# Reordering the first pieces of work of an attention and mixture kernel, and dropping a pause of three steps later on

## The chip, the cores and the metric

The kernel runs on one core of one Trainium2 chip. The time is the device time of one execution in microseconds (us). Five engines matter: TensorE (PE in the rows) multiplies matrices, VectorE (DVE), ScalarE (ACT) and GpSimd (POOL) work element by element, and SyncE (SP, SPq for its queue) starts the transfers of the DMA engines. Each engine executes its own list of instructions in a fixed order and waits, at the head of that list, for what the next instruction needs.

## The reference, cut to what matters

Inputs: q, k, v of shape (8, 8, 576, 64), p of shape (8, 8, 32, 64); weights of two feed-forward stages. All float32.

```python
def sm_attn(qq, kk, vv):
    s = scale * np.matmul(qq, kk.transpose(0, 1, 3, 2))
    s = s - np.max(s, axis=-1, keepdims=True)
    a = np.exp(s)
    a = a / (np.sum(a, axis=-1, keepdims=True) + 1e-09)
    return np.matmul(a, vv)
p_packed = sm_attn(p, k, v)              # packing: 32 rows a head
out = sm_attn(q, p_packed, p_packed)     # spreading: 576 rows a head
x = out.transpose(0, 2, 1, 3).reshape(4608, 512)
h = x @ w_in                             # 512 -> 2048
x = (h * (1.0 / (1.0 + np.exp(-h)))) @ w_out
a = x @ w1                               # 512 -> 1024
b = x @ w2
h = a * b @ w3
return h @ w_out2                        # 1024 -> 512
```

## The kernel before, in words

Stage 1 does attention and the first feed-forward part, batch by batch; stage 2, from about 826 us on, does the second part with factors that were stored in DRAM. This text touches two places: the start, before TensorE has its steady flow of products, and the first 100 us of stage 2.

**The start.** The string `START` (L70 to L76) lists pieces of work in the order in which the program records them, up to each `|`. `P0` and `P1` are steps of the packing of batch 0 and batch 1 (`Pack.steps`): scores into `ps_s` (L318), maximum (L449, L450), exponential (L454), transposes into `ps_t` (L467), their copies `e`, the product `ps_o` (L318), its scaled copies `pk` on ACT (L491), the transpose `pkT` on DVE (L496) and the blocks `sbd` on POOL (L268). `S0` and `S1` are steps of `Spread` (from L600) for one half of batch 0's rows: transpose of the scores (L606), maximum (L610), subtraction (L611), exponential (L614), sums (L617 to L619), multiplication (L620), transpose back `sT` (L625), and the split of it into `a2`. The spread of `S0` is marked `early`.

`F` is one step of the weight decoder: the weights come in as 64-bit words, and class `Decode` turns one 128x512 piece into floats with two copies on ACT (`ps_dec`, `raw`, by way of L82), two instructions on DVE (L190, L192) and an addition on POOL (L196). `L` starts the load of a piece (L214). The buffers of the pieces go round, so a load waits until POOL's addition of an earlier piece has ended. The first eight pieces (`zi`) are of the first weight matrix, those behind them (`z`) of the second. `D` is `direct0`: two matrix products (L700) of `zi` with batch 0's packed rows `mbd` into one PSUM bank `ps_m0`, which is split into the slots `mq`: the high part is a copy on ACT (L82), the low part a subtraction on DVE (L91). Once `a2` and `mq` are there, a loop over items runs: `ps_h` (L98 to L100), then sg (L882), gg (L887), gh and gl, then `ps_x`.

Each number that is multiplied is carried as two parts, high and low: `split_hi` is a copy on ACT (L82), `split_lo` a subtraction on DVE or POOL (L91).

A scheduler then sets each engine's final order. `tc.issue_after(behind[x])` (in `hold`, L104) tells it that an instruction is not to stand ahead of the recorded instruction `behind[x]`. `act_on` (from L806) runs the tokens; it holds an `F` behind the latest `sg` and `gg`, once there are any.

**Stage 2.** `emit_ab` records, per step, products of left and right factors into `ps_a`, `ps_b` and `ps_e` (L1393), sums of them on DVE (`y`, L1424), and `o_steps` (L1554) multiplies the results by `w`, with sums on DVE (`o`, L1536). A generator of side work, `first_group`, is advanced between them: `second_right_factors` prepares the factors `w` from `zz` in four rounds (`mp` 0 to 3), then `right_sums(1)` forms the sums `xt`, `x2r`, `zz` on POOL (L1206) for the next group of rows, and these are split into `xct` and `xcb`. The last right factors are needed when the next group starts at about 920 us. Before round `mp` = 2 there are three bare `yield`s (L1305, L1306).

## Time and profile before

| | |
|---|---|
| device time, median of three runs | 1382.71 us (1380.78 to 1382.86) |
| the profiled execution: its own time | 1379.92 us |
| its span in the trace | 1378.1 us |
| PE busy | 1348.4 us, 98% of the span, 9161 instructions |
| DVE busy | 933.8 us, 68% |
| POOL busy | 902.3 us, 65% |
| ACT busy | 728.5 us, 53% |
| mean granted clock of TensorE | 0.998 of full |
| bytes moved | 272.94 MB, 198 GB/s in the mean |

The span runs from the first to the last instruction of the trace; the execution's own time is 1.82 us longer. A share of busy time is a mean over the whole span. The first slice of 40 has PE at 7 tenths, the others are at 8 or 9 and above; how much an engine waits in a stretch is read from the rows of that stretch.

### The profile page before, as it was taken

Reading aid. Unit: us, or ns where it says so; the run is one execution under the profiler, and the core shown is the slowest. Engines: PE = TensorE matmul, PEld = TensorE weight load, DVE = VectorE, ACT = ScalarE, POOL = GpSimd, SP = SyncE. Lnnn points to the kernel's source line nnn. Section 1 sums busy time; section 2 is a strip of 40 time slices with the busy share of each in tenths; the row PEclk is TensorE's granted clock in tenths of the full one; section 3 lists DMA queues with packets and bytes.
Section 4 is the critical chain, followed back from the end, with each engine's and each line's share of the span. In section 5 each row is a group of like instructions: output and inputs, shape, how many; then the busy total and the mean of one; then the engine's idle time right before and its main releaser. Section 6 shows DMA issues by size and latency. Waiting matters only on the chain.

```text
span 1378.1 us, 26479 instructions
## 1 busy us (share of the span) xinstructions
PE 1348.4 (98%) x9161; PEld 1306.8 (95%) x9161; DVE 933.8 (68%) x1622; ACT 728.5 (53%) x1633; POOL 902.3 (65%) x866
## 2 busy tenths in 40 slices
PE   7899999999999999999999999999999999999998
PEld 5688899999999999999999999999999999999998
DVE  5874747369665578767669748885775757757665
ACT  5855756465675566665556636443334433333432
POOL 2875967666889677888567544593755747646632
PEclk9999999999999999999999999999999999999999
DMA  9588757534676454865547648656667576576751
GB/s 322 187 297 263 242 165 224 166 120 150 224 235 192 144 157 126 268 206 152 197 137 246 194 159 304 214 169 199 220 185 237 169 213 218 169 218 203 214 161 54
DMA packets 191557, 272.94 MB, mean 198 GB/s; under 512 B 18752, under 2 KB 112320, under 8 KB 191424
## 3 DMA queue, kind: packets, MB, share of 16 engines
q1 hardware_dynamic: 173168, 251.20, 58.5%
q10 hardware_dynamic: 18256, 20.06, 4.2%
q8 instruction: 73, 1.20, 0.4%
q14 instruction: 60, 0.49, 0.1%
HBM read 209.06 MB, written 62.13 MB: 197 GB/s over the span
## 4 chain that ended last, share of the span: by engine, by line
PE 84%; DVE 6%; ACT 3%; POOL 2%; DMA 2%; issue 2%; SPq 1%; DVEq 0%; ACTq 0%; POOLq 0%
PE ps_a L1393 13%; PE ps_o L1554 12%; PE ps_x L100 8%; PE ps_x L98 8%; PE ps_x L99 8%; PE ps_e L1393 7%; PE ps_h L98 4%; PE ps_h L100 4%; PE ps_h L99 4%; PE ps_b L1393 3%; PE ps_w L99 1%; PE ps_w L98 1%; PE ps_w L100 1%; PE ps_m L99 1%; PE ps_m L98 1%
## 5 line engine op out<-in xcount | busy, mean ns | idle before, releaser
L98 PE MATMUL ps_x<-gh,wo 128*128 128x288 f32 x1024 | 301.8, 297 | 1.3 <-DVE xs L924 1.3
L99 PE MATMUL ps_x<-gh,wo 128*128 128x288 f32 x1024 | 300.4, 295 | 0.0
L100 PE MATMUL ps_x<-gl,wo 128*128 128x288 f32 x1024 | 293.7, 298 | 0.0
L91 POOL TENSOR_TENSOR gl<-gg,gh 128x288 fp32r<-128x288 f32 x256 | 232.4, 910 | 83.1 <-ACT gh L82 62.0
L887 DVE SCALAR_TENSOR_TENSOR gg<-sg,ps_h 128x288 f32<-128x288 f32 x256 | 114.8, 448 | 177.6 <-ACT sg L882 109.2
L1536 DVE TENSOR_TENSOR o<-o,ps_o 128x768 f32<-128x768 f32 x137 | 130.0, 950 | 97.2 <-PE ps_o L1554 94.6
L98 PEld LDWEIGHTS ps_x<-gh,wo 128*128 128x128 f32 x1024 | 192.1, 188 | 3.9 <-DVE xs L924 1.5
L99 PEld LDWEIGHTS ps_x<-gh,wo 128*128 128x128 f32 x1024 | 192.3, 188 | 1.9 <-issue 1.1
L91 POOL TENSOR_TENSOR mq<-mr,mq 128x256 fp32r<-128x256 f32 x168 | 140.4, 837 | 79.1 <-DVE mq L830 43.9
L100 PEld LDWEIGHTS ps_x<-gl,wo 128*128 128x128 f32 x1024 | 188.6, 188 | 3.0 <-issue 2.2
L82 ACT ACTIVATE gh<-gg 128x288 fp32r<-128x288 f32 x256 | 113.0, 442 | 92.1 <-DVE gg L887 86.7
L882 ACT ACTIVATE sg<-ps_h 128x288 f32<-128x288 f32 x256 | 103.6, 405 | 107.1 <-PE ps_h L100 82.7
L98 PE MATMUL ps_h<-a,mq 128*128 128x288 f32 x512 | 154.6, 302 | 1.6 <-DVE gg L887 1.6
L100 PE MATMUL ps_h<-a,mq 128*128 128x288 f32 x512 | 151.8, 297 | 0.0
L99 PE MATMUL ps_h<-a,mq 128*128 128x288 f32 x512 | 151.4, 296 | 0.0
L91 POOL TENSOR_TENSOR lfa<-y,lfa 128x384 fp32r<-128x384 f32 x69 | 78.7, 1140 | 83.2 <-ACT lfa L82 73.9
L1554 PE MATMUL ps_o<-w,lfs 128*128 128x256 f32 x828 | 118.5, 282 | 0.0
L1393 PE MATMUL ps_a<-xct,ws 128*128 128x384 f32 x576 | 116.0, 335 | 0.0
L1554 PEld LDWEIGHTS ps_o<-w,lfs 128*128 128x128 f32 x828 | 112.2, 190 | 0.0
L98 PEld LDWEIGHTS ps_h<-a,mq 128*128 128x128 f32 x512 | 96.1, 188 | 7.1 <-DVE gg L887 2.9
L1393 PEld LDWEIGHTS ps_a<-xct,ws 128*128 128x128 f32 x576 | 99.9, 188 | 0.0
L99 PEld LDWEIGHTS ps_h<-a,mq 128*128 128x128 f32 x512 | 96.1, 188 | 3.4 <-issue 1.4
(225 smaller groups left out, 3177.9 us busy)
## 6 DMA issues: line engine op xcount, KB each, us to landing
ws<-w_d SPq DMA_DIRECT2D x192, 256.0 KB, 3.1
wa<-w_d SPq DMA_DIRECT2D x144, 256.0 KB, 3.0
mr<-m_d SPq DMA_DIRECT2D x144, 128.0 KB, 2.7
raw<-in_moe_w_dram SPq DMA_DIRECT2D x32, 512.0 KB, 4.6
w_d<-w12s ACTq DMA_DIRECT2D x56, 256.0 KB, 2.8
wz<-wi_d SPq DMA_DIRECT2D x48, 256.0 KB, 4.3
m_d<-ms SPq DMA_DIRECT2D x96, 128.0 KB, 3.2
x_d<-xs SPq DMA_DIRECT2D x20, 576.0 KB, 3.6
```

The costliest lines, as they stand in the source:

```text
L82: return A.activation(out=dst, in_=src, func=ACTF.Copy, scale=mul)
L91: (eng or V).tensor_tensor(out=lo, in0=src, in1=hi.bitcast(F32), op=ALU.subtract)
L98: T.matmul(out=dst, lhsT=wh, rhs=xh, start=start, stop=False)
L99: T.matmul(out=dst, lhsT=wl, rhs=xh, start=False, stop=False)
L100: return T.matmul(out=dst, lhsT=wh, rhs=xl, start=False, stop=stop)
L882: ins = A.activation(out=sg, in_=ps, func=ACTF.Tanh, scale=0.5)
L887: ins = V.scalar_tensor_tensor(out=gg, in0=sg, scalar=1.0, in1=ps, op0=ALU.add, op1=ALU.mult)
L1393: ins = T.matmul(out=bank, lhsT=w[:, kt, wp], rhs=xt[:, kt, xp], start=first and (kt, n) == (0, 0), stop=last and (kt, n) == (1, 2), skip_ ...
L1536: V.tensor_tensor(out=oacc[k], in0=oacc[k], in1=ps, op=ALU.add)
L1554: T.matmul(out=ps[:, t], lhsT=l[:, lp], rhs=w[:, wp], start=fresh and t != 1 and n == 0, stop=done and t != 0 and n == 2, skip_group_check ...
```

## The change

The first line of `START` that has `P0 P0 P0 P0` is put in another order, with the same nine `F`, eight `L` and two `D`. Three decodes now stand directly behind batch 0's packing, the first step of batch 1's packing stands between the two spread steps, and `D D` follows the fourth decode. Until `sg` exists, every `F` and every `P1` is held behind the latest recorded instruction of batch 0 on ACT (`first_a`) and on DVE (`first_v`). These are set by the copies `e` of batch 0's packing, by four places of the early spread and by `direct0`. The tile `sT` of the early spread comes from the pool of the gate tiles `gg` in place of the pool `work`. In stage 2 the three `yield`s go.

```diff
-        "P0 P0 P0 P0 P0.tail S0 S0 P1 F L F L S1.load S0 P1 F L F L D D P1 F L F L P1 F L F L F "
+        "P0 P0 P0 P0 P0.tail F L F L F L S0 P1 S0 F L S1.load S0 P1 D D F L P1 F L F L P1 F L F "
...
             for et, (r, cs) in zip(pts, self.PARTS):
-                split_hi(ep[0][0:r, cs], et)
+                x = split_hi(ep[0][0:r, cs], et)
+                if self.b == 0:
+                    behind.update(first_a=x.ins)
...
-            V.tensor_tensor(
+            x = V.tensor_tensor(
                 out=s, in0=s, in1=mx.unsqueeze(2).to_broadcast([128, n, 32]), op=ALU.subtract
             )
-            A.activation(out=s, in_=s, func=ACTF.Exp, scale=scale)
+            y = A.activation(out=s, in_=s, func=ACTF.Exp, scale=scale)
+            if self.early:
+                behind.update(first_v=x.ins, first_a=y.ins)
...
-            sT = work([128, n * 32], "sT")
-            V.transpose(out=sT, in_=s.rearrange("p k i -> p (k i)"))
+            if self.early:
+                sT = g_p.tile([128, HS], F32, tag="gg", name="sT", bufs=4)
+            else:
+                sT = work([128, n * 32], "sT")
+            x = V.transpose(out=sT, in_=s.rearrange("p k i -> p (k i)"))
             cols = slice(hv[0] * HS, hv[-1] * HS + HS)
-            split(a2[b][:, hg, 0, cols], a2[b][:, hg, 1, cols], sT, eng=G if self.early else V)
+            y = split_hi(a2[b][:, hg, 0, cols], sT)
+            split_lo(a2[b][:, hg, 1, cols], sT, a2[b][:, hg, 0, cols], G if self.early else V)
+            if self.early:
+                behind.update(first_v=x.ins, first_a=y.ins)
...
-        split(dst[:, :, 0], dst[:, :, 1], ps.rearrange("p (j f) -> p j f", j=4))
+        src = ps.rearrange("p (j f) -> p j f", j=4)
+        behind["first_a"] = split_hi(dst[:, :, 0], src).ins
+        behind["first_v"] = split_lo(dst[:, :, 1], src, dst[:, :, 0]).ins
...
-            with hold("sg", "gg") if token == "F" and "sg" in behind else ExitStack():
+            last = ("sg", "gg") if "sg" in behind else ("first_v", "first_a")
+            held = token == "F" or (token == "P1" and "sg" not in behind)
+            with hold(*[x for x in last if held and x in behind]):
                 act(token)
...
-            for _ in range(3 if mp == 2 else 0):
-                yield
```

The final order differs only in the first 88 us or so and between 826 and 930 us; in between and behind, every engine's list is the same.

**DVE at the second direct product.** Before, this piece of VectorE's list reads as follows. `zi2` and `zi3` are decoded weights, `mq_176<-ps_m0_470` is the low part of the second direct product, `sT` the transposes back of batch 0's spread.

```order
L190 TENSOR_SCALAR zi2_186<-ps_dec_491 128x512
L192 SCALAR_TENSOR_TENSOR raws_180<-ps_dec_491,raws_180 128x512
L620 TENSOR_TENSOR s2_352<-s2_352,sm_363 128x288
L190 TENSOR_SCALAR zi3_187<-ps_dec_520 128x512
L192 SCALAR_TENSOR_TENSOR raws_180<-ps_dec_520,raws_180 128x512
L476 TENSOR_REDUCE rs_392<-psum0_131 128x1
L477 RECIPROCAL rs_392<-rs_392 128x1
L496 STREAM_TRANSPOSE pkT_505<-pk_500 128x64
L625 STREAM_TRANSPOSE sT_417<-s2_343 128x288
L91 TENSOR_TENSOR mq_176<-ps_m0_470,mq_176 128x4x128
L625 STREAM_TRANSPOSE sT_421<-s2_352 128x288
```

And in the changed kernel:

```order
L189 TENSOR_SCALAR zi1_185<-ps_dec_422 128x512
L191 SCALAR_TENSOR_TENSOR raw_241<-ps_dec_422,raw_241 128x512
L633 STREAM_TRANSPOSE sT_437<-s2_374 128x288
L477 TENSOR_REDUCE rs_388<-psum1_132 128x1
L477 TENSOR_REDUCE rs_404<-psum0_131 128x1
L478 RECIPROCAL rs_388<-rs_388 128x1
L478 RECIPROCAL rs_404<-rs_404 128x1
L90 TENSOR_TENSOR mq_176<-ps_m0_470,mq_176 128x4x128
L189 TENSOR_SCALAR zi2_186<-ps_dec_475 128x512
L191 SCALAR_TENSOR_TENSOR raw_243<-ps_dec_475,raw_243 128x512
L189 TENSOR_SCALAR zi2_186<-ps_dec_491 128x512
```

The subtraction `mq_176<-ps_m0_470` now stands ahead of the decodes of `zi2` and `zi3`, where these stood ahead of it; both `sT` stand ahead of it.

**PE at the same product.** The same product on TensorE, whose second half is the last matrix product that the subtraction needs; before:

```order
L318 MATMUL ps_s_384<-rows1_194,pb_225 128x288 x2
L700 MATMUL ps_m0_470<-zi1_185,mbd_157 128x512
L318 MATMUL ps_s_387<-rows1_194,pb_225 128x288 x2
L467 MATMUL ps_t_426<-ident_60,e1_381 128x128 x3
L467 MATMUL ps_t_430<-ident_60,e1_381 96x128 x2
L318 MATMUL ps_o_475<-vz_229,e_425 128x256 x2
```

And in the changed kernel, up to the second half:

```order
L317 MATMUL ps_s_399<-rows1_194,pb_225 128x288 x2
L466 MATMUL ps_t_442<-ident_60,e1_393 128x128 x3
L466 MATMUL ps_t_446<-ident_60,e1_393 96x128 x2
L466 MATMUL ps_t_454<-ident_60,e1_409 128x128 x3
L466 MATMUL ps_t_458<-ident_60,e1_409 96x128 x2
L317 MATMUL ps_o_483<-vz_229,e_441 128x256 x2
L317 MATMUL ps_o_483<-vz_231,e_441 128x256
L711 MATMUL ps_m0_470<-zi1_185,mbd_157 128x512
```

Both halves of batch 1's transposes (`ps_t_442` to `ps_t_458`) now stand ahead of the second half of `ps_m0_470`; before, only one half of them did.

**SP at the loads of the next queries.** `kq` and `rows2` are the query rows that the spread `S1` needs. Before:

```order
L214 DMA raw_243<-in_moe_w_in_dram 128x512
L214 DMA raws_180<-in_moe_w_in_dram 128x512 x2
L115 DMA kq_414<-in_q_dram 128x2x288
L115 DMA rows2_192<-in_q_dram 128x2x288
L214 DMA raw_455<-in_moe_w_in_dram 128x512
L214 DMA raw_463<-in_moe_w_out_dram 128x512
```

And in the changed kernel:

```order
L213 DMA raw_243<-in_moe_w_in_dram 128x512
L213 DMA raws_180<-in_moe_w_in_dram 128x512 x2
L213 DMA raw_359<-in_moe_w_in_dram 128x512
L213 DMA raw_428<-in_moe_w_out_dram 128x512
L114 DMA kq_430<-in_q_dram 128x2x288
L114 DMA rows2_192<-in_q_dram 128x2x288
```

The two loads of queries moved behind two more loads of weights, which need freed buffers.

**POOL in stage 2.** Here `xt`, `x2r` and `zz` are the sums for the next group of rows, `w34_3` the last of the factors `w`, `xct` and `xcb` low parts of the right factors. Before:

```order
L1206 TENSOR_TENSOR xt_12751<-x2r_12379 128x768
L91 TENSOR_TENSOR lfa22_12652<-y122_12518,lfa22_12652 128x384
L91 TENSOR_TENSOR lfs3_12646<-tmp_12612,lfs3_12646 128x384
L91 TENSOR_TENSOR lfs2_12618<-tmp_12611,lfs2_12618 128x384
L1424 TENSOR_TENSOR tmp_12612<-y021_12393,tmp_12611 128x384
L1206 TENSOR_TENSOR x2r_12379<-x2r_12379 128x2x384
L91 TENSOR_TENSOR w34_3_12530<-zz_12254,w34_3_12530 128x256
L91 TENSOR_TENSOR lfa12_12649<-y021_12393,lfa12_12649 128x384
L91 TENSOR_TENSOR xct1_12789<-xt_12751,xct1_12789 128x2x384
L1206 TENSOR_TENSOR zz_12752<-x2r_12379,xt_12751 128x768
```

And in the changed kernel:

```order
L1221 TENSOR_TENSOR xt_12692<-x2r_12384 128x768
L90 TENSOR_TENSOR lfa22_12657<-y122_12525,lfa22_12657 128x384
L90 TENSOR_TENSOR lfs3_12651<-tmp_12616,lfs3_12651 128x384
L90 TENSOR_TENSOR lfs2_12622<-tmp_12615,lfs2_12622 128x384
L1437 TENSOR_TENSOR tmp_12616<-y021_12398,tmp_12615 128x384
L1221 TENSOR_TENSOR x2r_12384<-x2r_12384 128x2x384
L1221 TENSOR_TENSOR zz_12693<-x2r_12384,xt_12692 128x768
L90 TENSOR_TENSOR lfa12_12654<-y021_12398,lfa12_12654 128x384
L90 TENSOR_TENSOR xcb11_12767<-x2r_12384,xcb11_12767 128x2x384
L90 TENSOR_TENSOR lfs4_12647<-tmp_12616,lfs4_12647 128x384
```

The first `zz` moved up by three instructions: a `w34_3`, an `lfa12` and an `xct1` that stood between it and `x2r` now stand elsewhere.

## Rows read from the trace of the kernel before

**Rows 1.** Windows: busy us (instructions) of PE, PEld, DVE, ACT, POOL; clock, DMA share, GB/s.

```profile
15.89:55.67 39.78, 31.02 (x124) 21.47 (x125) 34.55 (x78) 34.42 (x86) 24.37 (x23) 0.96 0.71 244
...
80.00:122.00 42.00, 42.00 (x281) 38.22 (x280) 25.51 (x50) 25.05 (x56) 28.79 (x29) 1.00 0.82 265
```

**Rows 2.** Chain of waits that ended at 68 us: start, length in us, what.

```profile
57.64 1.31 POOL z L196
...
58.97 0.33 SPq L214
...
60.29 6.15 DMA kq<-in_q_dram
...
66.57 1.21 PE ps_s L318 x4
```

**Rows 3.** Timeline of ACT: start, us, engine, line, operation, [idle before <- releaser].

```profile
15.23 0.62 ACT L82 ACTIVATE ps_dec<-raws 128x512 f32<-128x512 f32 x1 [1.45 <-DMA raws<-in_moe_w_in_dram]
...
16.33 1.46 ACT L491 ACTIVATE pk<-ps_o,rs 32x128 f32<-32x128 f32 x4
...
27.86 0.50 ACT L454 ACTIVATE e<-ps_s,nb 128x288 f32<-128x288 f32 x1
...
31.36 0.75 ACT L82 ACTIVATE e<-ps_t 128x384 f32<-128x384 f32 x2
```

**Rows 4.** Timeline of DVE in the start.

```profile
15.89 0.69 DVE L190 TENSOR_SCALAR zi<-ps_dec 128x512 int32<-128x512 int32 x1 [1.71 <-ACT ps_dec L82]
...
35.41 0.68 DVE L192 SCALAR_TENSOR_TENSOR raws<-ps_dec,raws 128x512 int32<-128x512 int32 x1
...
37.02 0.43 DVE L625 STREAM_TRANSPOSE sT<-s 128x288 f32<-128x288 f32 x1
37.40 0.69 DVE L91 TENSOR_TENSOR mq<-ps_m,mq 128x512 fp32r<-128x512 f32 x1
...
55.67 0.45 DVE L887 SCALAR_TENSOR_TENSOR gg<-sg,ps_h 128x288 f32<-128x288 f32 x1
```

**Rows 5.** Timeline of PE in the start.

```profile
12.38 2.43 PE L318 MATMUL ps_o<-vr,e 128*128 128x256 f32 x10 [0.36 <-ACT e L82]
...
31.89 2.43 PE L318 MATMUL ps_o<-vz,e 128*128 128x256 f32 x10 [2.05 <-ACT e L82]
34.15 1.02 PE L700 MATMUL ps_m<-zi,mbd 128*128 128x512 f32 x2
```

**Rows 6.** Timeline of SP's queue: start, us, the issue of transfers.

```profile
23.75 0.55 SPq L115 DMA_DIRECT2D kq<-in_q_dram  x1
```

**Rows 7.** DMA issues: count, KB each, us to landing; 22 to 30, then 31 to 36 us.

```profile
kq<-in_q_dram SPq DMA_DIRECT2D x1, 288.0 KB, 7.6
...
raw<-in_moe_w_out_dram SPq DMA_DIRECT2D x2, 512.0 KB, 4.0
```

**Rows 8.** Windows of stage 2, columns as in rows 1.

```profile
920.00:928.00 8.00, 6.17 (x38) 5.15 (x36) 8.00 (x9) 3.10 (x6) 8.00 (x6) 1.00 0.45 133
```

**Rows 9.** Waits of PE, 900 to 940 us: total us, times, longest.

```profile
PE ps_a L1393 <- DVE y L1424: 0.8, 1, 0.8
PE ps_o L1554 <- DVE o L1536: 0.8, 1, 0.8
PE ps_e L1393 <- DVE xcb L91: 0.3, 1, 0.3
```

**Rows 10.** Timeline of DVE in stage 2.

```profile
915.00 2.70 DVE L91 TENSOR_TENSOR xct<-zz,xct 128x768 fp32r<-128x768 f32 x1 [1.15 <-ACT xct L82]
...
918.91 0.54 DVE L1424 TENSOR_TENSOR y<-p,ps_a 128x384 f32<-128x384 f32 x1
919.49 1.62 DVE L1424 TENSOR_TENSOR y<-y,y 128x384 f32<-128x384 f32 x1
```

**Rows 11.** Timeline of POOL in stage 2.

```profile
899.49 2.16 POOL L1206 TENSOR_TENSOR xt<-x2r 128x768 f32<-128x768 f32 x1
...
912.24 1.85 POOL L1206 TENSOR_TENSOR zz<-x2r,xt 128x768 f32<-128x768 f32 x1
```

More of the change, by code (lines that the diff above doesn't have):

```diff
@@ L85, in split_hi @@
         if on_vector:
-            V.tensor_copy(out=hi, in_=src)
-        else:
-            act_copy(hi, src)
+            return V.tensor_copy(out=hi, in_=src)
+        return act_copy(hi, src)
     def split_lo(lo, src, hi, eng=None):
-        (eng or V).tensor_tensor(out=lo, in0=src, in1=hi.bitcast(F32), op=ALU.subtract)
+        return (eng or V).tensor_tensor(out=lo, in0=src, in1=hi.bitcast(F32), op=ALU.subtract)
     def split(hi, lo, src, on_vector=False, eng=None):
@@ L619, in steps @@
             V.reciprocal(out=sm, in_=sm)
-            V.tensor_tensor(
+            x = V.tensor_tensor(
                 out=s, in0=s, in1=sm.unsqueeze(2).to_broadcast([128, n, 32]), op=ALU.mult
             )
+            if self.early:
+                behind.update(first_v=x.ins)
             yield
-            sT = work([128, n * 32], "sT")
-            V.transpose(out=sT, in_=s.rearrange("p k i -> p (k i)"))
+            if self.early:
[3 more added lines that the diff above has]
+            x = V.transpose(out=sT, in_=s.rearrange("p k i -> p (k i)"))
             cols = slice(hv[0] * HS, hv[-1] * HS + HS)
-            split(a2[b][:, hg, 0, cols], a2[b][:, hg, 1, cols], sT, eng=G if self.early else V)
+            y = split_hi(a2[b][:, hg, 0, cols], sT)
+            split_lo(a2[b][:, hg, 1, cols], sT, a2[b][:, hg, 0, cols], G if self.early else V)
+            if self.early:
+                behind.update(first_v=x.ins, first_a=y.ins)
             yield
```

## The prediction

> **What bounds the kernel now.** I read the page's shares first (PE busy for 98% of the span), then windows, to find where PE is not full. There are two places in reach of the change. In the first, the start, the reader is to see that from 15.89 to 55.67 us PE is busy 31.02 of 39.78 us and loses 8.76, while DVE is busy 34.55 and ACT 34.42 [rows 1]. Both are nearly full: the start is a queue of work on two engines, and what it ends with is what it has packed plus what it idled, 5.23 us on DVE. From 80 to 122 us PE is full in all 42 us [rows 1], so a start that ends later or earlier passes on what it gained or lost. The chain of waits says how: POOL's addition of the fifth piece of the second weight matrix at 57.64 us frees the buffer for the load that SP issues at 58.97, the query load behind it on SP's queue is under way from 60.29 for 6.15 us, and PE's `ps_s` at 66.57 waits for it [rows 2]. In the second place, 920 to 928 us, PE is busy 6.17 of 8 us [rows 8] and loses 1.83; its waits are for DVE three times, 0.8, 0.8 and 0.3 us, together 1.9 [rows 9]. DVE and POOL are both busy for all 8 us there [rows 8]. Everywhere else the lists of all engines are the same, so the sum is that of these two places.
>
> **The start, part by part.** Nothing is added or removed: the same nine decodes, two packings and two spread halves, and `sT` only lies in another buffer. So the packed work of DVE to the third `gg`, 34.55 us, stays, and I work out its start and its idle time.
>
> *The start.* Before, ACT took the first decode's copies at 15.23, when the load had landed, and the scaled copies `pk` behind them at 16.33, for 1.46 us [rows 3]. In the changed order `pk` is first. Its input, the first `ps_o`, ends at 12.38 + 2.43 = 14.81 us [rows 5], so DVE gets its first instruction (the transpose of `pk`) at about 14.86 + 1.46 + 0.03 = 16.35, against 15.89 [rows 4]: 0.46 later. The first spread step comes out of it much earlier: by the same walk the first `sT` ends at about 26.2 us where it began at 37.02 [rows 4], and the first `ps_h` would go at 27.5.
>
> *The idle time.* The first decode stands behind `pk` and two copies `e` and starts on ACT at 17.1; with 0.62 us for `ps_dec` [rows 3] DVE has it at 17.7 after an estimated wait of 1.12 us. Four hand-overs in the spread and the packing I put at 0.2, 0.5, 0.15 and 0.55 by the like ones of before. The large term is new. DVE's list now has the subtraction `mq` of the second direct product ahead of the decodes of `zi2` and `zi3`, and PE's list has all ten transposes of batch 1 ahead of that product's second half. My walk: batch 1's fourth maximum ends at about 29.8, its `nb` on ACT at 30.45; four exponentials, of 0.50 us each [rows 3], go to 32.55; the copy of `sT` to 33.0, two pairs of copies `e` at 0.75 a pair [rows 3] to 34.5. PE starts `ps_o` behind the first pair, and three of its products, 0.43 each by their spacing within such a group, end at 34.75; the half of `ps_m` adds 0.43 and ends near 35.2; ACT copies its high part until 35.8; DVE subtracts at 35.85. DVE has nothing else in its list from about 33.25: 2.6 us idle, and the decodes behind it, three of which were done by 36.1 before [rows 4], start at 35.9 on ACT. Behind that lie 0.65 and 0.25 us for `pk` and for the last split of `a`. Together 1.12 + 1.4 + 2.6 + 0.9 = 6.0 us of idle, against 5.23.
>
> *The sum of the start.* 16.35 + 34.55 + 6.0 = 56.9 us for the third `gg`, against 55.67 [rows 4]: +1.2. The same walk puts POOL's fifth piece at 58.9 to 59.4 us against 57.64 [rows 2], which is +1.3 to +1.8. I take +1.3.
>
> *The bounds.* If the hand-overs fall so that the second half of `ps_m` is ready when DVE comes to it, the 2.6 us go and the start is 1.3 us shorter; with the small waits kinder too, -1.5. On the other side is SP: the loads of the next queries go from 23.75 us [rows 6] to a place behind two weight loads, the second of which needs POOL's fourth addition, at about 33.4. They are issued near 33.9 and wanted by PE near 38.5. In the crowded stretch from 22 to 30 us such a load took 7.6 us to land; two loads of 512 KB issued from 31 to 36 us took 4.0 [rows 7]. I take 4.0 (fewer loads are under way at 34 us), so 37.9, and nothing is lost; by 7.6 it is 41.5 and 3.0 us are. So the start lies between -1.5 and +4.3.
>
> The other edits: holding `P1` and `F` behind batch 0's instructions costs what the walk says, as the wait is only a place in the list; `sT` in a gate tile costs nothing, since four buffers are there and the first `gg` needs one only at about 46 us, 20 us after the first `sT`. If that cover went, a `gg` would wait for POOL's low part of `a`, about 0.8 us.
>
> **Stage 2, part by part.** Three bare steps less before `mp` = 2 let the side work be recorded three places earlier, not run less. In POOL's list the first sum `xt` keeps its place behind the same `tmp`, so it starts at 899.49 as before [rows 11]; but the first `zz`, at 912.24 [rows 11], loses three instructions ahead of it (a `w34_3` split, an `lfa12` and an `xct1`). I put its end at about 910.3 in place of 914.1. DVE's `xct<-zz`, which waited 1.15 us for ACT's copy of it [rows 10], then waits no more, and from 915.0 to 928.4 DVE was never idle: what it starts earlier it ends earlier. That gives -1.15 of the 1.9 us that PE waits for DVE [rows 9]. All the work of POOL and DVE is still there, so I take -1.1. Bounds: all 1.9 us go, at best; at worst the split that DVE did at 915 meets POOL's in another order and PE waits 1 us more.
>
> Row first for the one rule that speaks against this: `y<-p,ps_a`, with one input in PSUM, takes 0.54 us while POOL is full, and `y<-y,y`, half a microsecond later with two inputs in SBUF, 1.62 [rows 10]. By the Trainium skill, page "SBUF — State Buffer", section "Who interferes with whom", a DVE instruction with two SBUF inputs and a GpSimd instruction that reads SBUF exclude each other for as long as one lasts. The trace agrees with it in these two rows.
>
> **The sum.** +1.3 - 1.1 = +0.2 us: 1380.1 for an execution like the profiled one (1379.92), which was 2.79 us under the median. On the median it is 1382.71 + 0.2 = 1382.9 us. What the measurement tells from no change is 0.2%, about 2.8 us.
>
> **The rivals.**
>
> *A. The second direct product is ready in time.* Then the start gains 1.3 us, and with all 1.9 us of stage 2 the sum is -3.2: 1379.5 us. For it: the first `sT` is 11 us earlier, and the first two items wait only for `mq`, so PE gets its first `ps_x` sooner. Against it: ten transposes and two pairs of copies `e` must pass ahead of it, and `ps_o` waited 2.05 us for such copies before [rows 5].
>
> *B. The late queries.* PE's scores of `S1` stand ahead of the other `ps_h`; if the query load lands after 7.6 us in place of 4.0, PE and behind it DVE lose 3.0 us, the start is +4.3, the sum +3.2: 1385.9 us. From a landing time of about 7.2 us on the kernel is slower by more than 0.2%. For it: 7.6 us at 23.75, and 6.15 at 60.29 [rows 2, 7]. Against: 4.0 at 31 to 36 us.
>
> *C. Stage 2 only moves its crowd.* `y<-y,y` pays 1.08 us over the 0.54 of its neighbour [rows 10]; if what POOL does earlier only meets other instructions of DVE with two inputs, and they stretch by as much, DVE's list ends no earlier and the gain is 0: +1.3, 1384.0 us. Against it: the 1.15 us ahead of `xct` are a wait for a result of ACT, not for POOL. This is what the skill's rule on the shared port would make of it.
>
> **How the numbers follow.** Forecast 0.38 (of this 0.05 faster and 0.05 slower by over 0.2%, 0.28 the same, from the bounds of its terms); A 0.25 (0.19 faster, 0.06 same); B 0.20 (0.15 slower, 0.05 same); C 0.17 (0.01 faster, 0.11 same, 0.05 slower). Faster 0.25, same 0.50, slower 0.25. The forecast's own range is 1381.0 to 1385.0. The lowest sum of the bounds is -1.5 - 1.9 = -3.4, or 1379.3, the highest +4.3 + 1.0 = +5.3, or 1388.0; with half a microsecond for the runs' own spread below, and the top of B's tail left out, the range is 1378.8 to 1386.8.
>
> **What would show it.** Right: the first `ps_h` before 29 us; a wait of DVE of about 2.6 us ahead of the subtraction `mq` near 35.8, released by ACT; the query load issued at about 33.9; the third `gg` at 56.9; `ps_s` that waits for the second query load at 67.9 in place of 66.57; in stage 2 the first `zz` on POOL near 908.5 on the old scale, no wait ahead of `xct<-zz`, and less than 1 us of PE's waits for DVE at 920 to 928. Wrong: the third `gg` before 55 us, or a PE that waits for `kq` near 40 us; a longer stretch at a low granted clock in the first 60 us; PE's waits in stage 2 at another step, after 928 us.

## The result and the profile after

The changed kernel is slower: 1389.54 us (median of five runs, 1388.97 to 1392.45) against 1380.78 us for the kernel before in the same session (1379.04 to 1382.86); the ratio is 1.0055, 95% interval 1.0042 to 1.0068. In a later session (e8 below) it was 1.0048 (1.0030 to 1.0065). The forecast was 1382.9, with a range up to 1386.8. It is wrong, and mainly in the start.

Where the time goes is read by following one and the same matrix product through both traces. Its start is later in the changed kernel by 3.9 us at 60 us, 7.8 at 80, 8.9 at 130, 9.5 at 820, 9.3 at 1000 and 9.6 at 1370. So in this profile the start loses nearly all of it, and stage 2 gives nothing back. In e8's profile, the same kernel, the shift is 5.1 at 94 us, 4.5 at 190 and 8.0 at 1370; what is added behind the start is of the size by which runs of one kernel differ.

The start as one window, from DVE's first instruction to the third `gg`, with the columns of [rows 1]:

```profile
15.71:61.39 45.68, 37.92 (x136) 24.60 (x136) 36.77 (x79) 35.97 (x86) 25.50 (x23) 0.89 0.65 219
32.00:36.00 4.00, 3.93 (x15) 2.91 (x14) 1.64 (x7) 2.91 (x11) 2.04 (x2) 0.57 0.20 46
48.00:52.00 4.00, 4.00 (x5) 1.78 (x6) 3.85 (x11) 3.95 (x9) 2.65 (x4) 0.50 0.79 241
72.00:76.00 4.00, 3.17 (x11) 2.73 (x12) 1.19 (x3) 1.22 (x4) 4.00 (x4) 0.66 1.01 396
```

The same three short windows before:

```profile
32.00:36.00 4.00, 4.00 (x17) 3.00 (x18) 3.81 (x9) 3.99 (x12) 3.21 (x3) 1.00 0.61 153
48.00:52.00 4.00, 4.00 (x9) 1.85 (x8) 4.00 (x10) 3.64 (x11) 3.66 (x4) 0.63 0.31 104
72.00:76.00 4.00, 4.00 (x26) 3.44 (x25) 3.25 (x8) 3.65 (x8) 1.41 (x3) 1.00 1.02 372
```

Against the first of [rows 1] DVE starts 0.18 us earlier, is idle 45.68 - 36.77 = 8.91 us in place of 5.23, and its packed work is 36.77 in place of 34.55: -0.18 + 3.68 + 2.22 = +5.7, which is the third `gg` at 61.39 against 55.67. The clock stands at 0.57 of full from 32 to 36 us (before: 1.00), at the half level of 1.2 GHz all through 48 to 52 (before: 0.63), and at 0.66 from 72 to 76 (before: 1.00).

Of these terms only the longer idle time is in all profiles of this start. The same window in e8 and in e2 (the kernel that has only the start changed), each up to its own third `gg`:

```profile
15.90:60.56 44.66, 36.68 (x127) 23.11 (x127) 34.97 (x79) 34.66 (x84) 24.50 (x23) 0.89 0.65 223
```

```profile
15.21:59.41 44.20, 36.24 (x127) 23.28 (x127) 34.93 (x79) 34.62 (x84) 24.48 (x23) 0.88 0.67 227
```

DVE is idle there for 9.69 and 9.27 us, but its packed work is 34.97 and 34.93, 0.4 above before; 36.77 is this one execution's.

DVE's timeline shows both losses. The second row answers to the fourth of [rows 4]; the columns are start, length, operation, and idle time before it with what ended it:

```profile
27.52 0.48 DVE L607 STREAM_TRANSPOSE s<-ps_s 128x288 f32<-128x288 f32 x1 [1.14 <-PE ps_s L317]
...
38.04 0.69 DVE L90 TENSOR_TENSOR mq<-ps_m,mq 128x512 fp32r<-128x512 f32 x1 [4.41 <-ACT mq L82]
...
53.04 1.50 DVE L623 TENSOR_TENSOR s<-s,sm 128x288 f32<-128x288 f32 x1
...
58.52 2.94 DVE L90 TENSOR_TENSOR a<-sT,a 128x288 fp32r<-128x288 f32 x2
61.39 0.44 DVE L902 SCALAR_TENSOR_TENSOR gg<-sg,ps_h 128x288 f32<-128x288 f32 x1
```

DVE waits 4.41 us ahead of the held subtraction (4.64 in e8, 4.24 in e2), and 1.14 us for the scores of the spread's second half. The two subtractions `a<-sT` take 2.94 us together; as groups of lines, before and after, they are:

```profile
L91 DVE TENSOR_TENSOR a<-sT,a 128x288 fp32r<-128x288 f32 x2 | 1.1, 556 | 0.8 <-ACT a L82 0.8
```

```profile
L90 DVE TENSOR_TENSOR a<-sT,a 128x288 fp32r<-128x288 f32 x2 | 2.9, 1510 | 0.0
```

What is beside them is on POOL, additions and splits without a gap:

```profile
55.66 2.74 POOL L90 TENSOR_TENSOR wo<-z,wo 128x512 fp32r<-128x512 f32 x2
58.36 1.31 POOL L195 TENSOR_TENSOR z<-z,raws 128x512 int32<-128x512 int32 x1
59.62 1.52 POOL L90 TENSOR_TENSOR wo<-z,wo 128x512 fp32r<-128x512 f32 x1
```

Each `a<-sT` lasts about as long as the POOL instruction that runs with it. Both have two inputs in SBUF. The Trainium skill, page "SBUF — State Buffer", section "Who interferes with whom", has such a pair exclude each other; these rows agree, 1510 against 556 ns. In e8 and e2 only the second of the two is stretched (0.66 and 1.56 us, 0.65 and 1.56).

Why the subtraction is late is read on PE, with the rows that answer to [rows 5]. A product of `ps_s`, `ps_o` or `ps_m` stands there as two records, a transpose as one:

```profile
31.78 2.44 PE L466 MATMUL ps_t<-ident,e 128*128 128x128 f32 x10 [2.48 <-ACT e L453]
34.25 2.27 PE L317 MATMUL ps_o<-vz,e 128*128 128x256 f32 x6
36.35 1.02 PE L711 MATMUL ps_m<-zi,mbd 128*128 128x512 f32 x2
...
47.96 6.07 PE L711 MATMUL ps_m<-zi,mbd 128*128 128x512 f32 x8 [2.11 <-DVE gg L902]
...
72.83 1.84 PE L317 MATMUL ps_s<-kq,sbd 128*128 128x288 f32 x4 [2.57 <-ACT gh L82]
```

The trace before has the same pattern once, at the second of these places:

```profile
46.70 2.95 PE L700 MATMUL ps_m<-zi,mbd 128*128 128x512 f32 x4 [2.56 <-DVE gg L887]
```

Four records (two halves of a direct product) took 2.95 us there, behind 2.56 us of idle time, and the clock from 48 to 52 us was 0.63. In the changed kernel TensorE idles 2.48 us before the transposes, then ten of them take 2.44 us in the stretch at 0.57, and the second half of the direct product ends near 37.3. The second idle time, 1.82 and 2.11 us around 45 us, goes with a longer stretch at half clock, in which eight records of `ps_m` take 6.07 us. The third one, 2.57 us, comes before the scores of the late queries at 72.83 (66.57 in [rows 2]). There the lateness of the third `gg` reaches TensorE, by the chain of [rows 2]: POOL's addition of the fifth piece (57.64 there) and the query load behind it (60.29 there) are both 5.5 us later:

```profile
63.16 1.33 POOL L195 TENSOR_TENSOR z<-z,raw 128x512 int32<-128x512 int32 x1 [2.02 <-PE ps_h L99]
```

```profile
65.84 1.43 SPq L114 DMA_DIRECT2D kq<-in_q_dram  x2
```

The load lands at 72.7. In e8 (the row below) and e2 TensorE's wait at this place is 2.26 and 2.23 us, and the load itself ends it:

```profile
71.70 1.21 PE L317 MATMUL ps_s<-kq,sbd 128*128 128x288 f32 x4 [2.26 <-DMA kq<-in_q_dram]
```

The scores are 6.3 us later than before here, 5.1 in e8 and 3.9 in e2, and the shift of TensorE's products at 80 us is 7.8, 5.1 and 3.9. The 1.5 us by which the first of these exceeds the lateness of the scores are the fall of the clock behind the wait (0.66 from 72 to 76 us); it comes and goes, for in e8 it isn't there (1.00).

Stage 2 is as crowded as it was. PE's waits, against [rows 9]:

```profile
PE ps_o L1567 <- DVE o L1549: 1.5, 1, 1.5
PE ps_e L1406 <- ACT p L82: 0.3, 1, 0.3
PE ps_e L1406 <- DVE xcb L90: 0.2, 1, 0.2
```

```profile
923.77 1.76 DVE L90 TENSOR_TENSOR xct<-zz,xct 128x768 fp32r<-128x768 f32 x1 [0.76 <-ACT xct L82]
```

The 0.8 us for `y` are gone, those for `o` grew from 0.8 to 1.5: together 2.0 against 1.9. `xct<-zz` begins 0.4 us earlier on the old scale (923.77 less 9.2 is 914.6, against 915.00 in [rows 10]). From the 5660th to the 6400th product TensorE takes 116.04 us before and 116.16 after. (TensorE's order differs from before up to 957 us, not only to 930, and at the start up to 101; both lie inside the stretches that are compared here.) In the second profile of the changed kernel (e8) it takes 117.6: there the clock falls behind the same wait of 1.5 us, which it doesn't in the first. The 10 us from the end of that wait on, which is at 938.07 in after and at 934.15 in e8:

```profile
938.00:948.00 10.00, 9.93 (x68) 9.93 (x69) 6.61 (x11) 3.45 (x7) 5.82 (x6) 1.00 0.45 131
```

```profile
934.00:944.00 10.00, 9.85 (x56) 9.86 (x57) 5.84 (x10) 2.95 (x6) 5.86 (x6) 0.83 0.36 103
```

In e8 these 10 us hold 56 records of products in place of 68, at 0.83 of the full clock.

### The profile page after: what moved, and what is told of

The parts are those of the page before. It is cut to its first block, busy times and chain, and to the rows that moved or that the text cites. A ratio compares the mean times of both kernels' runs of the same rounds, so it can differ in the third digit from the quotient of the medians.

```text
span 1387.8 us, 26487 instructions
## 1 busy us (share of the span) xinstructions
PE 1354.5 (98%) x9161; PEld 1309.0 (94%) x9161; DVE 933.9 (67%) x1622; ACT 727.8 (52%) x1633; POOL 900.9 (65%) x866
## 4 chain that ended last, share of the span: by engine, by line
PE 84%; DVE 6%; ACT 3%; DMA 2%; issue 2%; POOL 2%; SPq 1%; DVEq 0%; ACTq 0%; POOLq 0%
PE ps_a L1406 13%; PE ps_o L1567 11%; PE ps_x L99 8%; PE ps_x L97 8%; PE ps_x L98 8%; PE ps_e L1406 6%; PE ps_h L97 4%; PE ps_h L99 4%; PE ps_h L98 4%; PE ps_b L1406 3%; PE ps_w L97 1%; PE ps_w L98 1%; PE ps_w L99 1%; DMA m_d<-ms 1%; DVE y L1437 1%
```

## The experiments

Each was timed against the kernel before on the same chip; given are the ratio to it with its 95% interval, and the median in us. The medians of before were 1382.1 to 1382.9 in the five sessions.

**e1, the changed kernel without direct0's hold.** Nothing else is changed.

```diff
-        behind["first_a"] = split_hi(dst[:, :, 0], src).ins
-        behind["first_v"] = split_lo(dst[:, :, 1], src, dst[:, :, 0]).ins
+        split_hi(dst[:, :, 0], src)
+        split_lo(dst[:, :, 1], src, dst[:, :, 0])
```

> The changed kernel, but direct0 no longer sets first_a and first_v, so the fifth to eighth decode may stand ahead of the subtraction mq of the second direct product; in VectorE's order they do. In the changed kernel VectorE waited 4.41 us ahead of that subtraction (33.6 to 38.0 us) and ScalarE 2.30 us, with the decodes behind it. Theory 1 (the hold behind direct0 makes that wait, and the wait is on the path): the wait is filled with decodes, the third gg comes at 57 to 59 us in place of 61.4, and the time falls by 3 to 4.5 us against the changed kernel, to about 1385 to 1386. Theory 2 (the clock makes the start longer, and the wait is only where it shows): TensorE still idles before 31.8 us and its clock falls, ten transposes still take 2.4 us; less than 1.5 us comes back.

0.9997 (0.9987 to 1.0008), 1383.05: the whole loss is gone. The decodes fill the wait, the subtraction comes later (41.23) and harms nobody, the third `gg` is at 56.36:

```profile
34.82 0.69 DVE L189 TENSOR_SCALAR zi<-ps_dec 128x512 int32<-128x512 int32 x1 [1.37 <-ACT ps_dec L82]
...
41.23 0.68 DVE L90 TENSOR_TENSOR mq<-ps_m,mq 128x512 fp32r<-128x512 f32 x1
...
56.36 0.45 DVE L902 SCALAR_TENSOR_TENSOR gg<-sg,ps_h 128x288 f32<-128x288 f32 x1
...
59.36 2.15 DVE L90 TENSOR_TENSOR a<-sT,a 128x288 fp32r<-128x288 f32 x2
```

The order changed in one more respect: both `a<-sT` now stand behind the third `gg`, which they no longer hold up. TensorE's clock still falls from 32 to 36 us (0.58) and from 48 to 52 (0.50), so these falls cost little on this order: e10 below, the same kernel with the first of them gone, is 0.05% under it. The query load goes out at 61.04 here, and the scores of the late queries are at 66.43, without a wait.

**e2, only the start**: the changed kernel with the pause put back.

```diff
+            for _ in range(3 if mp == 2 else 0):
+                yield
```

> The changed kernel with the three bare steps before round 2 of the right factors put back, so only the start is changed. In the profiles of the two kernels the shift of TensorE's products was 9.5 us just before stage 2's first products (at 830 us) and 9.3 at 940, so by theory 1 (stage 2 gains next to nothing) the time is that of the changed kernel within 0.5 us, about 1389.5. By the forecast's own sum (1.1 us gained in stage 2) it is 1.1 us longer, 1390.6.

1.0034 (1.0021 to 1.0047), 1387.15. **e4, only stage 2**: the kernel before with the same two lines taken out.

> The kernel before with only the three bare steps ahead of round 2 of the right factors taken out; the start is as before. Theory 1 (stage 2 gains next to nothing; from the shift of TensorE's products, 9.5 us at 830 and 9.3 at 940): same as before within 0.7 us. Theory 2 (the forecast): 1.1 us shorter.

1.0010 (1.0000 to 1.0021), 1383.98. No gain of 1.1 us in either; the missing pause costs a little. All profiles together say how. In the five with the pause (before, e2, e5, e14, e16) PE waits 0.8 us for `y` and 0.8 for `o`, and takes 116.04 to 116.08 us from the 5660th to the 6400th product. In the fifteen without it, it waits once, 1.5 or 1.6 us for `o`: eleven take 116.1 to 116.2 us, and four (e8, e3_fill10, e6, e13) 117.6 to 117.7, with the clock at 0.83 in the 10 us behind that wait, as shown for e8. So the missing pause costs 0.1 us, and 1.6 in about one profile of four; from these counts I estimate 0.5 us in the mean. e4's +0.10%, e17 against e16 (+1.7 us on the medians) and e8 against e2 (1.0048 and 1.0034, on two chips) have the same sign, none of them clear by itself.

**e3_fill10, e3_fill24, e6 and e7, idle transposes that missed the gap.** TensorE was to be kept busy before 31.8 us:

```diff
+                if b == 1 and r == 128 and hg == 0:
+                    for _ in range(10):
+                        T.transpose(pt[:, 0:128], ident, ident)
```

> The changed kernel with 10 idle transposes of the identity on TensorE ahead of batch 1's first transposes (they write a bank that the real ones overwrite), about 1.1 us of work in a gap of about 2.5 us. The order changes with it in one respect: the second half of the second direct product now stands ahead of batch 1's ps_o. It is the control of the next kernel, which has the same order up to ps_o. Theory 1 (the idle gap before 31.8 us lowers the clock): if 10 are too few, the clock still falls, the ten real transposes take about 2.4 us, and the subtraction mq comes near 36 us; time 1387 to 1388. Theory 2 (no effect of the clock, order alone): same time as with 24.

> As the kernel before, with 24 idle transposes, about 2.6 us of work, which fill the gap between the fourth score product (29.3 us) and the first real transpose (31.8 us). Theory 1 (the clock): the granted clock stays at its full level from 32 to 36 us, the ten transposes take 1.2 us in place of 2.4, the subtraction mq comes near 34.5 us, and the time is 1.5 to 2 us below that with 10 idle transposes. Theory 2 (order alone): the two agree within 0.5 us, whatever the clock does, since VectorE and ScalarE have other work to do.

In e6 (the changed kernel) and e7 (e1) they were to go to a bank of their own, behind the fourth maximum of the scores:

```diff
+            if b == 1 and hg == 0:
+                idle = bank("idle")
+                with hold("scored"):
+                    for _ in range(20):
+                        T.transpose(idle[:, 0:128], ident, ident)
```

> The changed kernel with 20 idle transposes of the identity on TensorE, now into a free bank, so that they can run in the gap between the fourth score product of batch 1 (29 us) and its first transpose (31.8 us), about 2.3 us of work; the earlier fillers waited for the bank of the scores and came behind the gap. The scheduler answers by putting the second half of the second direct product ahead of ps_o and of the last two transposes. Theory 1 (the half clock behind the gap makes the subtraction mq late): the granted clock stays full from 32 to 36 us, the subtraction comes near 35.5 us in place of 38.0, and the time falls to 1385 or below. Theory 2 (the hold costs whatever the clock does): the subtraction comes earlier but the time stays above 1386, since the decodes still stand behind it.

> The same fillers in the kernel without direct0's hold (e1_direct_free). Theory 1 (clock and hold both cost, and add up): 1 to 2 us below e1_direct_free, about 1381.5, so below the kernel before. Theory 2 (with the hold gone TensorE's products of the first 55 us are not on the path): within 0.7 us of e1_direct_free, about 1383.

1.0011 (1.0001 to 1.0022), 1.0017 (1.0005 to 1.0029), 1.0013 (1.0002 to 1.0025) and 1.0002 (0.9990 to 1.0014). As a test of the clock all four failed: the bank they wrote to was still held by the scores, in e6 and e7 too, so they ran behind the idle gap and ahead of the real transposes, as in e6:

```profile
31.94 3.48 PE L465 MATMUL idle<-ident 128*128 128x128 f32 x20 [2.49 <-ACT e L455]
```

In e3_fill24 the clock held even so, and the ten real transposes took 1.26 us, but they came only at 34.99. The subtraction came no earlier (37.6 to 38.4 us in the three with the hold), yet by their ratios these three are 4 to 6 us faster than the changed kernel. The scheduler had answered the extra work with another order, so they can't tell the clock from the order.

**e8, the changed kernel again, and e9, e10 with fillers that hit the gap**: a bank that is free, and the place in PE's list right behind the fourth score product.

```diff
+            if b == 1 and hg == 0:
+                idle = acc_bank(1, "idle")
...
```

> The changed kernel itself, beside the next three on one chip. It was 0.55% slower than before in its first runs, and the kernel that differs from it in stage 2 alone (e2_start_only) 0.34% on another day. Theory 1 (the clock's fall at 72 to 76 us, seen in the changed kernel's profile and not in that of e2_start_only, comes and goes with the run): between 0.35 and 0.55% here. Theory 2 (stage 2 without its pause costs 2 us or more, against what its profile shows): 0.55% again, and the others without the pause slow as well.

> The changed kernel with 20 idle transposes, this time in a bank that nothing else holds and ordered right behind batch 1's fourth score product, without a wait: they run inside the gap (29.3 to 31.8 us). TensorE's order of everything else up to the second direct product is that of the changed kernel. Theory 1 (the half clock behind the gap makes the late subtraction later): the clock is full from 32 to 36 us, ten transposes take 1.2 us in place of 2.4, the subtraction mq comes at 35.9, as the forecast had it, and the time is 1.5 to 3 us below the changed kernel. Theory 2 (the clock is harmless, the hold alone costs): the subtraction comes 2 us earlier and the time is the same within 1 us.

> The same fillers in the kernel without direct0's hold. Theory 1: with the hold gone the path no longer runs through those products, time within 1 us of e1_direct_free, about the time before. Theory 2 (clock and hold add up): 1.5 us or more below the kernel before.

e8 1.0048 (1.0030 to 1.0065), 1388.69; e9 1.0013 (1.0000 to 1.0026), 1384.29; e10 0.9992 (0.9982 to 1.0001), 1381.66. In e9 the clock holds, as its windows show:

```profile
28.00:32.00 4.00, 3.95 (x28) 3.27 (x26) 3.69 (x13) 2.02 (x6) 0.38 (x1) 1.00 0.65 259
32.00:36.00 4.00, 3.14 (x17) 1.99 (x16) 2.29 (x8) 3.56 (x13) 2.04 (x2) 1.00 0.03 5
...
48.00:52.00 4.00, 3.75 (x6) 1.76 (x7) 4.00 (x10) 3.24 (x8) 2.98 (x4) 0.60 0.75 235
```

4.4 us came back on the same chip, but not by the way that I expected: the wait ahead of the subtraction is still 3.70 us (4.41), since PE now waits for the exponentials and the copies `e` of ACT:

```profile
32.43 1.99 PE L473 MATMUL ps_t<-ident,e 128*128 128x128 f32 x10 [0.30 <-ACT e L455]
34.90 1.56 PE L317 MATMUL ps_o<-vz,e 128*128 128x256 f32 x6 [0.47 <-ACT e L82]
36.30 1.02 PE L718 MATMUL ps_m<-zi,mbd 128*128 128x512 f32 x2
```

And here, too, both `a<-sT` moved behind the third `gg` (57.27). The query load goes out as late as in the changed kernel (66.05), but TensorE has other products ahead of the scores (71.64) and doesn't wait for them.

**e5, the hold alone in the kernel before**: direct0's two lines and the hold of `F`, nothing else.

```diff
+        behind["first_a"] = split_hi(dst[:, :, 0], src).ins
+        behind["first_v"] = split_lo(dst[:, :, 1], src, dst[:, :, 0]).ins
...
-            with hold("sg", "gg") if token == "F" and "sg" in behind else ExitStack():
+            last = ("sg", "gg") if "sg" in behind else ("first_v", "first_a")
+            with hold(*[x for x in last if token == "F" and x in behind]):
```

> The kernel before with one part of the change alone: direct0 sets first_a and first_v, and each decode that is recorded behind it, until sg exists, is held behind them. START, the packing, the spread and stage 2 are as before. In VectorE's list the subtraction mq of the second direct product then stands ahead of the decodes of zi2 and zi3. Theory 1 (this hold is the part that costs): VectorE idles for 2 us or more ahead of the subtraction, the third gg comes 3 us or more later than 55.7, and the time is 3 to 6 us longer than before. Theory 2 (it costs only together with the new START and the earlier spread): within 1.5 us of before.

1.0011 (0.9999 to 1.0023), 1384.52. DVE waits 1.57 us, not for the subtraction but for the transpose of `pk` ahead of it, which is at 35.32; the subtraction follows at 35.88. The third `gg` is 3.4 us late here (59.11), with both `a<-sT` ahead of it and the clock at half from 48 to 52 us, and the time is still only 0.1% longer; TensorE doesn't wait for the scores of the late queries (68.67). The hold alone does not cost what it costs with the new START.

**e11, the new START without the new holds.** `F` is held as in the kernel before, `P1` not at all.

```diff
-            with hold(*[x for x in last if held and x in behind]):
+            with hold("sg", "gg") if token == "F" and "sg" in behind else ExitStack():
```

> The changed kernel with no hold before sg exists: START in its new order, sT in the gate tile, no pause, but F and P1 as free as before. Theory 1 (only direct0's hold costs, the other holds and the new START are neutral): the time of e1_direct_free, within 0.1% of before. Theory 2 (the new START itself costs, or the holds of P1 and of the first F gain): 0.15% or more above e1_direct_free.

1.0013 (1.0001 to 1.0025), 1383.74, the third `gg` at 56.75. A small loss, or none, is all that the new START costs when nothing is held; it is no gain either.

**e12, e13, e14, the second gap filled** (43.4 to 47.6 us in the changed kernel, 44.1 to 46.7 before):

```diff
+            if b == 1:
+                for _ in range((17, 17)[self.hg]):
+                    T.transpose(ps, ident, ident)
             T.transpose(ps, self.pk.rearrange("p y d -> p (y d)"), ident)
```

> The changed kernel with 17 idle transposes ahead of each of batch 1's two transposes ps_pk, in the same banks, so that TensorE is busy from 43.4 to about 47.6 us, where it idled 1.82 and 2.11 us; the first gap stays. Theory 1 (the second half-clock stretch is what makes the third gg late, by making the third and fourth direct product late): the clock is full from 47.6 us on, eight halves of ps_m take 3.5 us or less in place of 6.1, the third gg comes at 58 to 59 us in place of 60.6 to 61.4, and the time is 2 to 4 us below the changed kernel. Theory 2 (the first stretch counts): within 1 us of the changed kernel.

> The kernel without direct0's hold and with the first gap filled (e10), and with the fillers of e12 in the second gap too. Theory 1: another 1 to 2 us below e10, so 0.15% below before. Theory 2 (with the hold gone VectorE and ScalarE are the limit, not the products): within 0.7 us of e10.

> The kernel before with 20 idle transposes ahead of the transpose ps_pk of batch 1's second half, in the gap from 44.1 to 46.7 us (2.56 us), behind which its clock stood at half for 3.4 us (47.6 to 51.0). Theory 1 (the half clock costs there as it does in the changed kernel): 1 us or more below before. Theory 2 (in before VectorE was busy without pause there, so the products were not on the path): within 0.7 us.

e12 1.0005 (0.9995 to 1.0016), 1383.80; e13 1.0035 (1.0021 to 1.0048), 1387.42; e14 0.9987 (0.9975 to 0.9999), 1380.25. In e12 the clock is full from 40 us on, and eight records of `ps_m` take 3.67 us in place of 6.07:

```profile
49.56 3.67 PE L714 MATMUL ps_m<-zi,mbd 128*128 128x512 f32 x8 [0.27 <-DVE gg L905]
```

```profile
39.60 0.69 DVE L90 TENSOR_TENSOR mq<-ps_m,mq 128x512 fp32r<-128x512 f32 x1 [5.08 <-ACT mq L82]
...
59.20 0.41 DVE L905 SCALAR_TENSOR_TENSOR gg<-sg,ps_h 128x288 f32<-128x288 f32 x1
...
62.30 0.60 DVE L90 TENSOR_TENSOR a<-sT,a 128x288 fp32r<-128x288 f32 x1
```

This run refutes "the late subtraction alone": it waits longer here than in the changed kernel, 5.08 us, and nearly all the loss is gone. One of the two `a<-sT` stands behind the third `gg` and takes 0.60 us, the other, behind the fourth, 0.70. In e14's profile the clock holds from 48 to 52 us (1.00), but it is at half from 18.7 to 22 us, behind an idle stretch of 3.26 us which is 2.49 before; so the fall has moved and isn't gone. e13 is a miss that is explained only in part: its start is as good as that of e10 (third `gg` 57.20 and 57.52), its profile is 1.4 us behind e10's at 190 us and 5.1 at the end, and the medians are 5.8 apart. The first 1.4 us come with a fall of the clock behind a wait of 1.88 us (0.57 from 134 to 138 us, in e10 1.00), 1.5 more with the fall in stage 2; where the rest goes stays open.

**e15, D D ahead of P1, the hold kept.**

```diff
-F L S1.load S0 P1 D D F L P1
+F L S1.load S0 D D P1 F L P1
```

> The changed kernel with one exchange in START: D D ahead of the P1 that stood before it. The hold stays; TensorE's list now has the second half of the second direct product ahead of ps_o, and VectorE's has the subtraction right behind the second sT. Theory 1 (what costs is how late the held subtraction comes): the subtraction at 36 to 37 us, time 2 to 4 us below the changed kernel. Theory 2 (the hold costs by being there): within 1 us of the changed kernel.

1.0010 (1.0001 to 1.0018), 1383.72: the subtraction at 36.56 after a wait of 3.42 us, the `a<-sT` behind the third `gg`.

**e16 and e17, e14 again, and e14 without the pause.**

> The kernel before with 20 idle transposes in the gap from 44.1 to 46.7 us, a second time. Theory 1 (the half clock behind that gap costs): again 0.1% or more below before. Theory 2 (the first result was chance): within 0.05%.

> The same kernel without the three bare steps in stage 2. Theory 1 (the crowd in stage 2 only moves, and the missing pause costs 1 to 2 us): 0.07 to 0.2% above e16. Theory 2 (the forecast): 1.1 us, 0.08%, below e16. If the two agree within 0.05%, the pause is worth nothing either way.

e16 0.9995 (0.9984 to 1.0006), 1381.77; e17 1.0002 (0.9989 to 1.0015), 1383.49. The gain of e14 over the kernel before is not confirmed: 0.13 and 0.05%. Without the pause the median is 1.7 us longer.

## Why the prediction was wrong, step by step

**The start without the stage 2 term: expected +1.3 us, measured +5.7 at the third `gg` and 4.5 to 8.9 behind it.** The step that failed is the sum 16.35 + 34.55 + 6.0 = 56.9, and in it the idle term of 6.0: it was 8.91 (9.69 in e8, 9.27 in e2). The first term was 0.64 too long (15.71). Of the 8.91 the wait ahead of the subtraction is 4.41, forecast 2.6, and the rest 4.50, forecast 3.4; the largest piece of this rest is the 1.14 us for the scores at 27.52, where the largest of the four hand-overs was put at 0.55.

The walk to the subtraction had the right place, the right releaser and the right order. The 1.81 us that it missed are of three kinds. First the clock, about 0.7: the walk took each product at the length of the trace before, though by its own times TensorE has nothing to do between the last scores, whose maximum ends at 29.8, and the first exponential, which ends near 31, and the trace before has a fall of the clock behind an idle stretch of 2.56 us. With the clock kept full (e9) the wait was 3.70; the three products of `ps_o` ahead of the half of `ps_m` take 2.10 us from start to start at the lower clock (34.25 to 36.35) and 1.40 in e9. Second a reading, 0.6: the half of `ps_m` was priced at 0.43 us, which is one of its two records; in [rows 5] it takes 1.02, and so it does in both kernels here. The other 0.5 are hand-overs, above all that of ACT's copies `e` to `ps_o`: it starts 0.62 us behind DVE's last instruction both at the lower clock and in e9, and 0.2 in the walk (34.75 - 3 x 0.43 = 33.46 against 33.25, which is ahead of the end of the first pair of copies, 33.75).

**"The packed work of DVE stays, 34.55 us": nearly, in two profiles of three.** It was 34.97 in e8 and 34.93 in e2, but 36.77 in the first one, with the same instructions. There the decodes that were put off have POOL's additions and splits run beside the subtractions of the spread; the two `a<-sT` are 1.8 of the 2.2 us. I weighed the rule on the shared port for stage 2 alone, as rival C, and not for the start. With 0.4 us of longer work in place of 2.2, e8 and e2 are slower than before all the same.

**How the loss goes on from the third `gg`** was in the prediction, by the chain of [rows 2], with `ps_s` at 67.9 us. The chain held and was mis-sized with the start: `ps_s` came at 72.83 (71.70 in e8, 70.50 in e2), 2.2 to 2.6 us after TensorE had run out of work. The sign of being wrong that was named, a longer stretch at a low clock in the first 60 us, came true: the mean clock there was 0.91, before 0.97.

**What the loss is made of is settled in part.** Shown: direct0's hold is necessary for it (e1: all of it gone with two lines), it is not sufficient (e5: 0.1%), and neither the long wait (e12 has a longer one), nor the half clock (e1 has it, twice), nor a late third `gg` (59.20 in e12, 59.11 in e5) costs much by itself; with the third `gg` at 59.41 e2 loses 0.34%, e12 and e5 with nearly the same 0.05 and 0.11%. Three profiles of the changed start (after, e8, e2) have all of these together, both `a<-sT` ahead of the third `gg`, and the wait of 2.2 to 2.6 us for the scores of the late queries; no other kernel here with the new START has that wait. Each single repair (e1, e9, e12, e15) brings the time to within 0.13% of before, but in each of them the scheduler also moved the `a<-sT` behind the third `gg` and the scores to a place where TensorE doesn't wait for them, so the runs do not tell how much of the rest is the clock, how much the order and how much the late load. A kernel with the changed order in which only the two `a<-sT` or only the query load is moved was not run.

**Rivals.** A (the product in time) did not come; B neither: the query load was issued at 34.72, against the forecast 33.9, landed in 4.8 us, and PE had it at 40.24 without a wait for it; the load that came late was the next one. C was right about the size in stage 2, no gain: the forecast's -1.1 us was +0.1 us of TensorE's time (+1.6 in e8), and the wait for `o` took the place of that for `y`. That it is POOL's and DVE's shared port which sees to this was not tested. The `zz` did move forward (907.7 on the old scale, forecast 908.5) and the wait ahead of `xct` did shrink (1.15 to 0.76), but what DVE starts earlier there is not what PE waits for next. The step "what it starts earlier it ends earlier" failed.

**A start that is late stays late**: right. From 80 to 122 us PE is full in both, and the shift is handed on.

## What to carry to other kernels

A hold that names the latest recorded instruction also puts behind it everything that the queue had to fill its wait with. Before adding one, look at what that instruction waits for, and at what else the engine could do meanwhile. Where a walk through a new order leaves TensorE idle for as long as a stretch after which its clock fell in the old trace, the products behind the gap are to be priced at both clock levels. A term that one execution shows is to be looked for in a second one: 2.2 us of longer DVE work were in one profile of three. And when an experiment adds an instruction to a kernel whose order a scheduler makes, compare the orders first: here the answer of the scheduler could be as large as the effect that was to be measured.

## What was not expected of the hardware

A wait of 1.5 us was followed by a fall of the clock in some executions and not in others, of the same kernel too. In stage 2 two waits of 0.8 us left the clock at 1.00 in five profiles of five, one wait of 1.5 us in eleven of fifteen; in the other four it was 0.83 over the next 10 us, and TensorE took 1.5 us longer. That the division of the idle time makes the difference is not shown: if a fall came in 4 of 15, five profiles without one would still come up about one time in five (an estimate from these counts).

An idle gap of the same length is not followed by the same clock: behind 2.48 us of idle time before 31.8 us the clock was at 0.57 in the changed kernel, but in e3_fill24, with 2.48 us of idle before 32.3 and its 24 idle transposes right behind, at 1.00 throughout 32 to 36 us. And a full clock need not make an earlier result: in e9 the ten transposes still took 1.99 us (2.44), because they waited for ACT, and `ps_o` started no earlier behind DVE's last instruction than at the lower clock; what came back was 0.7 us, in `ps_o` itself.
